# Batch 1 of a fused retention and gated-MLP kernel: its MLP by halves of 256 tokens, its second half of attention in 64-token chunks

## The chip, the cores and the metric

The kernel runs on one core of a Trainium2 chip. The core has a matrix engine (PE, with its weight loads shown apart as PEld), a vector engine (DVE), a scalar engine (ACT), a general engine (POOL) and an engine that issues transfers (SP). Each engine works through its own instructions in order and waits on semaphores for the others. Matrix results land in PSUM, which has eight banks of 512 float32 columns per partition. The metric is the device time of one execution in microseconds.

## The reference, cut to what matters

```python
# q, k, v: (8 batches, 8 heads, 576 positions, 64)
scores = q @ k.T / sqrt(64)
gamma  = 1 - 2 ** (-5 - arange(8))                 # one decay per head
ret    = scores * where(i >= j, gamma ** (i - j), 0)
x      = (ret @ v)  laid out as (8 * 576 tokens, 512)
h      = x @ w_in                                   # (512, 2048)
g      = h / (1 + exp(-beta * h))                   # beta: one per column
out    = g @ w_out                                  # (4608, 512)
```

The decay is split: queries are multiplied by gamma^i and the scale, values by gamma^-j, so only the triangle (i >= j) has to be masked. This also lets everything before a chunk be summed up in a state, keys^T times values, one 64 x 64 block per head.

## The kernel before, in words

Each batch has a main block of 512 tokens; the 64 tokens left over of all eight batches form a ninth block. So there are nine blocks of 512 tokens for the MLP (called MoE in the names). For one block `up` (L542) computes one of 16 column groups `fo` of the hidden layer: four matmuls of 128 x 512 over `ko`, then a Silu on ACT from PSUM into `gT`. `down` (L575) does four of sixteen `fo` steps for one of four groups `ms` of 128 tokens; after the last of them the result is copied into `ot` and sent out. A block is thus 16 up steps and 16 down steps.

Main blocks hold their tokens interleaved by four: token 4*s + i lies in column s of group i. Queries are loaded that way (`load_q`, L73), so a chunk of 128 tokens is columns 32c to 32c+31 of all four groups.

Attention has two forms. Batches 0 and 1 work in 128-token chunks, `i` = 0 to 7 in `seq`: `a_sc` (scores, then the mask `causal` on DVE), `a_st` (adds to the running state in PSUM and copies it out to `sbds`), `a_O` (masked scores times values), `a_cross` (queries times the state), `a_x` (copy to `xT`, the MLP's input). Queries and keys are turned by PE (`t_q`, L317; `t_k`, L324). Batches 2 to 7 work in 64-token chunks, eight to a block, four small 64 x 64 matmuls at a time: `d_st` (L473) computes the states of four chunks into two banks, one of the tag st and one of the tag mm; its `chain` adds them up on DVE, four links, each with a cast on ACT into `sbq`. `d_sc` (L451) computes the scores with masks from `tri`; `d_out` (L494) the outputs and the cross terms, then evicts to `xT`. `scores(u)` and `outputs(u)` (L725, L732) put these together; `outputs(u)` holds the first states of batch u+1 between the two parts of the cross terms. Queries and keys of these batches are turned by transposing transfers on SP.

PSUM banks are shared by tag: mm has three (ups, downs and one bank of each `d_st`), O two, sc two, st one. A bank is given back, in program order, after the last use of what it held, and the bank that came back first is handed out next; the engine that writes it again waits on a semaphore until the last reader is done.

The order of work is written by hand. `fill` is the list of MLP steps; `merged` (L602) walks it, and before step n it issues every attention step whose time is at most n. `d0` is the first down of batch 0, `u1` the first up of batch 1 (d0 + 16), `base[n]` the first step of block n (`base[1]` is u1 + 10). In the kernel before, batch 1's list is 20 half-width ups (`fo` 0 to 9, tokens 0 to 255, then 256 to 511), six full ups and 16 downs: 42 steps. Chunks 4 and 5 are done at d0 + 12.7 to d0 + 15.9, chunks 6 and 7 among the half-width ups (u1 + 1 to u1 + 7), the first states of batch 2 (`early_states`) alone at u1 + 27, its scores and second states at base[2] - 10 and its outputs at base[2] - 3.5, all three among the downs.

SP issues in program order: queries, keys and values of batch 0, the weights, then queries, keys and values of batch 1, then those of batch 2, and so on.

Of the kernel before, what the change touches and what calls it, by code (L numbers as in the profile page):

```python
# [19 lines left out]
def kernel(  # L20
# [49 lines left out]
    QB = 2  # L70
    q_tiles, kv_tiles = {}, {}

    def load_q(b, us=(0, 1)):  # L73
# [51 lines left out]
    pos = consts.tile([P, 2, CB + 1], F32, name="pos")  # L125
    for j, (step, mul) in enumerate(((1, CB), (P, 1))):
        nc.gpsimd.iota(pos[:, j, :CB], pattern=[[step, CB]], base=0, channel_multiplier=mul,
                       allow_small_or_imprecise_dtypes=True)
        for x in range(2):
            nc.gpsimd.iota(pos[x * TL:(x + 1) * TL, j, CB:], pattern=[[0, 1]], base=MB, channel_multiplier=1,  # L130
                           allow_small_or_imprecise_dtypes=True)
    lscale = consts.tile([P, 1], F32, name="lscale")
    nc.vector.memset(lscale[:], math.log(scale))
    lg = consts.tile([P, 2, CB + 1, H], F32, name="lg")
# [5 lines left out]
    nc.scalar.activation(gv[:], lg[:, 1], ACT.Exp, scale=-1.0)  # L140

# [10 lines left out]
    tri = [consts.tile([P, TL], BF16, name=f"tri{i}") for i in range(2)]  # L152
# [97 lines left out]
    def head_of(b, p, j):  # L250
        return 2 * p + (j if b is not None and b < QB or p < 2 else 1 - j)

    def pre_q(b, n):
# [4 lines left out]
        if b < 2:  # L258
# [14 lines left out]
    def pre(i, js=(0, 1)):  # L273
# [22 lines left out]
        for to, hs in turned if b >= QB else [(slice(0, H), slice(0, H))]:  # L296
# [19 lines left out]

    def t_q(b, u):  # L317
# [12 lines left out]
    def q_cols(i, r, p):  # L330

        b, c = seq[i]
        if b is None:
            return live[i]["qkT"][r, 0, p, :], lambda o: o
        return (batch[b]["qT"][r, :, p, c * PC:(c + 1) * PC], lambda o: o.rearrange("k (i s) -> k i s", i=CB))

    def a_sc(i):
# [11 lines left out]
        m_b = causal[:].unsqueeze(1).to_broadcast([P, HP, P])  # L349
# [48 lines left out]
    def a_x(i):  # L398
        b, c = seq[i]
        x, view = xt(b)[:, :, :, c * PC:(c + 1) * PC], lambda o: o.rearrange("k p (i s) -> k p i s", i=CB)  # L400
        Os = live[i]["O"]
# [6 lines left out]
    def a_st(i):  # L408
# [11 lines left out]
        for j in range(2):  # L420
            r, cols = slice(j * D, (j + 1) * D), slice(j * D, (j + 1) * D)
            e = nc.vector.tensor_copy if i in (CB + 2, CB + 3) else nc.scalar.copy
# [4 lines left out]
            e(ends[b][(1 - j) * D:(2 - j) * D, 2:], st[r, 2:, cols])  # L427

# [9 lines left out]
    def q_of(u, c, j, p):  # L438

        if u == B:  # L440
            return piece(u, c)["qkT"][half(j), 0, p, half(c % 2)]
        w = TL // CB
        return batch[u]["qT"][half(j), :, p, c * w:(c + 1) * w]

    def columns(u, o):
        return o if u == B else o.rearrange("k (i s) -> k i s", i=CB)
# [4 lines left out]
    def d_sc(u):  # L451

        R = [sb.tile([P, 2, 2, HP, TL], BF16, name="R", tag="R", bufs=4) for _ in range(2)]
        sc = {}
        for x in range(2):
            for j in range(2):
                sc[x, j] = psum.tile([P, 2, HP, TL], F32, name="sc", tag="O" if x else "sc", bufs=2)
# [6 lines left out]
        mask = tri[1 if u == B else 0][:].unsqueeze(1).to_broadcast([P, 2 * HP, TL])  # L464
# [343 lines left out]
```

## Time and profile before

| | us |
|---|---|
| median of 3 runs (lowest, highest) | 299.39 (298.9, 300.13) |
| profiled execution, its span | 298.64, 296.9 |
| PE busy | 286.9 (97%) |
| ACT, POOL, DVE busy | 147.1, 109.0, 101.3 |
| an up or down step of 512 columns (four matmuls) | 0.86 |
| first up of batch 1, of batch 2, of batch 3 | 50.3, 84.2, 114.5 |

The granted clock of PE is 0.999 of full speed. A matmul's duration in the rows is longer than its share of PE's time, since matmuls overlap: 379 ns for one of 512 columns, but 0.215 us from one to the next. So steps are best measured from start to start, or by the chain of work in order of time. In a row the first number is the start, the second the length, both in us from the start of the span; a bracket at the end gives the engine's idle time ahead of it and what ended it. L549 is the MLP's up matmul, L551 its Silu, L582 the down matmul, L589 the copy of its result, L480 and L488 the states and the links of their sum, L491 the casts of these on ACT, L462 and L469 the 64-token scores and masks, L508, L521 and L536 the outputs, cross terms and evictions; L347, L351, L418, L394, L380 and L406 are the same for 128-token chunks.

### The profile page before, as it was taken

What the parts mean: (1) busy time and instruction counts of PE and PEld (TensorE: products, weight loads), DVE (VectorE), ACT (ScalarE), POOL (GpSimd) and SP (SyncE); (2) the same over time, 40 slices, a digit from 0 to 9 for tenths busy, and PEclk for the clock granted to TensorE, in tenths of its full rate; (3) what the DMA queues carried; (4) which work ended last, traced back from release to release, by engine and by line L of the source; (5) the groups of instructions that cost most, each with busy time, mean ns of one, the idle gap of its engine ahead of it and who ended that gap; (6) DMA issues with size and microseconds to landing.
All of it is one profiled execution on the core that took longest, in us unless ns stands there. A gap on an engine that the chain in (4) does not pass through costs nothing.

```text
span 296.9 us, 7459 instructions
## 1 busy us (share of the span) xinstructions
PE 286.9 (97%) x3147; PEld 149.2 (50%) x3177; DVE 101.3 (34%) x209; ACT 147.1 (50%) x257; POOL 109.0 (37%) x211
## 2 busy tenths in 40 slices
PE   7799999999999999999999999999999999999995
PEld 5554456855544454455445544554454544444444
DVE  5563656704640552045204530354054300120012
ACT  5567546683277434743484347433770157008600
POOL 3666107693750923370429216736223000000000
PEclk9999999999999999999999999999999999999999
DMA  8999999999999999949999849999976110131012
GB/s 213 218 333 393 386 273 252 224 203 222 252 169 254 270 196 242 242 68 160 233 237 207 178 99 272 195 181 188 205 168 140 73 38 0 35 71 38 0 71 73
DMA packets 128273, 53.97 MB, mean 182 GB/s; under 512 B 110048, under 2 KB 120688, under 8 KB 128240
## 3 DMA queue, kind: packets, MB, share of 16 engines
q1 hardware_dynamic: 128208, 53.49, 82.4%
q8 instruction: 25, 0.41, 0.6%
q14 instruction: 8, 0.07, 0.1%
q10 hardware_dynamic: 32, 0.01, 0.0%
HBM read 36.71 MB, written 9.44 MB: 155 GB/s over the span
## 4 chain that ended last, share of the span: by engine, by line
PE 83%; DMA 5%; SPq 5%; POOL 3%; issue 2%; ACT 1%; POOLq 0%; DVE 0%
PE po L582 38%; PE ph L549 33%; PE ph L564 4%; DMA tln<-in_k_dram 3%; SPq L94 2%; DMA kvn<-in_k_dram 2%; PE O L508 1%; SPq L113 1%; POOL kn L286 1%; PE st L480 1%; PE sc L462 1%; DMA kT<-kn 1%; SPq L305 1%; POOL kn L285 1%; PE O L521 1%
## 5 line engine op out<-in xcount | busy, mean ns | idle before, releaser
L582 PE MATMUL po<-w_out_sb,gT 128*128 128x512 bf16 (+2 forms) x590 | 125.6, 367 | 2.3 <-issue 2.1
L551 ACT ACTIVATE gT<-ph,beta_sb 128x512 bf16<-128x512 f32 (+1 forms) x140 | 91.2, 657 | 52.1 <-PE ph L549 51.7
L549 PE MATMUL ph<-xT,w_in_sb 128*128 128x512 bf16 (+1 forms) x550 | 114.5, 364 | 0.5
L582 PEld LDWEIGHTS <-gT 128*128 128x128 bf16 x608 | 56.9, 98 | 62.9
L549 PEld LDWEIGHTS <-w_in_sb 128*128 128x128 bf16 x560 | 54.3, 98 | 57.6 <-DVE sum L488 0.7
L589 DVE COPY ot<-po 128x512 f32<-128x512 f32 (+2 forms) x34 | 22.3, 657 | 72.3 <-PE po L582 71.6
L297 POOL CAST kn<-kvn 128x128 bf16<-128x128 f32 (+2 forms) x80 | 25.9, 359 | 43.5 <-DMA kvn<-in_k_dram 43.0
L266 POOL TENSOR_TENSOR qs<-qn,gq 128x256 bf16<-128x256 f32 (+1 forms) x36 | 26.3, 759 | 36.0 <-DMA qn<-in_q_dram 34.6
L469 DVE TENSOR_TENSOR R<-sc,tri 128x512 bf16<-128x512 f32 x28 | 17.4, 683 | 61.4 <-PE sc L462 61.4
L277 POOL TENSOR_TENSOR vn<-kvn,gv 128x512 bf16<-128x512 f32 x32 | 33.3, 1044 | 13.5 <-DMA kvn<-in_v_dram 8.5
L536 ACT CAST xT<-O 128x512 bf16<-128x512 f32 x14 | 7.5, 589 | 32.0 <-PE O L521 32.0
L491 ACT CAST sbd<-warm 128x256 bf16<-128x256 f32 x18 | 7.3, 405 | 25.5 <-DVE warm L488 20.6
L564 PE MATMUL ph<-xT,w_in_sb 128*128 128x512 bf16 x54 | 12.3, 379 | 0.3 <-ACT xT L404 0.2
L351 DVE TENSOR_TENSOR R<-sc,causal 128x512 bf16<-128x512 f32 x16 | 10.2, 685 | 4.6 <-PE sc L347 4.5
L488 DVE TENSOR_TENSOR sum<-st,warm 128x256 f32<-128x256 f32 x24 | 10.2, 425 | 2.5
L488 DVE TENSOR_TENSOR warm<-st,sum 128x256 f32<-128x256 f32 x18 | 7.6, 422 | 9.6 <-PE st L480 8.4
L536 DVE CAST xT<-O 128x512 bf16<-128x512 f32 x14 | 9.0, 686 | 5.0 <-PE O L521 5.0
L567 ACT ACTIVATE gT<-ph,beta_sb 128x512 bf16<-128x512 f32 x14 | 8.7, 687 | 4.2 <-PE ph L564 4.2
L285 POOL TENSOR_TENSOR kn<-tln,gq 128x128 bf16<-128x128 f32 (+1 forms) x12 | 5.7, 472 | 10.5 <-DMA tln<-in_q_dram 6.9
L194 POOL CAST w_in_sb<-wt 128x256 bf16<-128x256 f32 (+1 forms) x12 | 7.4, 623 | 4.9 <-DMA wt<-in_moe_w_in_dram 4.9
L564 PEld LDWEIGHTS <-w_in_sb 128*128 128x128 bf16 x56 | 5.4, 98 | 6.7 <-issue 0.3
L219 PE MATMUL ph<-warm 128*128 128x128 f32 (+1 forms) x24 | 7.3, 444 | 1.3 <-DVE warm L123 1.3
(81 smaller groups left out, 154.1 us busy)
## 6 DMA issues: line engine op xcount, KB each, us to landing
qn<-in_q_dram SPq DMA_DIRECT2D x16, 512.0 KB, 5.4
kvn<-in_k_dram SPq DMA_DIRECT2D x32, 256.0 KB, 5.4
kvn<-in_v_dram SPq DMA_DIRECT2D x32, 256.0 KB, 5.0
out_dram<-ot SPq DMA_DIRECT2D x31, 256.0 KB, 3.8
wt<-in_moe_w_out_dram SPq DMA_DIRECT2D x8, 512.0 KB, 9.1
wt<-in_moe_w_in_dram SPq DMA_DIRECT2D x5, 512.0 KB, 8.1
wt<-in_moe_w_in_dram SPq DMA_DIRECT2D x6, 256.0 KB, 5.5
out_dram<-ot SPq DMA_DIRECT2D x9, 128.0 KB, 2.4
```

The source lines that it names most:

```text
L266: nc.gpsimd.tensor_tensor(batch[b]["qs"][:, cs, to], q_tiles[b][:, hs, cs].rearrange("p h i d -> p i h d"), gq[:, cs, hs].unsqueeze(3).to_ ...
L277: nc.gpsimd.tensor_tensor(live[i]["vn"][:], kv_tiles.pop(i)[:, 1], gains(gv, c), ALU.mult)
L297: nc.gpsimd.tensor_copy(kn[:, c % 2, to], t[:, 0, hs])
L351: nc.vector.tensor_tensor(R[:, j], sc[j][:], m_b, ALU.mult)
L469: nc.vector.tensor_tensor(R[x][:, j].rearrange("k c p q -> k (c p) q"), sc[x, j].rearrange("k c p q -> k (c p) q"), mask, ALU.mult)
L488: nc.vector.tensor_tensor(new[:], add, sums[(c - 1) % 2][:], ALU.add)
L536: (nc.scalar.copy if n % 2 else nc.vector.tensor_copy)(x, o)
L549: nc.tensor.matmul(ph, w_in_sb[:, ko, fo * P:(fo + 1) * P], xts[m][:, ko, :, w], start=(ko == 0), stop=(ko == KO - 1))
L551: nc.scalar.activation(gts[m][:, fo, :, w], ph, ACT.Silu, scale=beta_sb[:, fo:fo + 1])
L564: nc.tensor.matmul(phs[f][:], w_in_sb[:, ko, f * P:(f + 1) * P], xts[m][:, ko], start=(ko == 0), stop=(ko == KO - 1))
L582: nc.tensor.matmul(po[:, :nn], gT[:, fo, ms, :], w_out_sb[:, fo, n0:n0 + nn], start=(fo == 0), stop=(fo == FO - 1))
L589: (nc.scalar.copy if m == 0 else nc.vector.tensor_copy)(ot, po[:, :nn])
```

## The change

Batch 1 (`HB`) is laid out by halves: token 256*x + 2*p + i lies in column p of group 2x + i. Its queries are loaded by halves of 256 tokens, in pieces of 512 bytes where they were 1 KB; the first half of its keys and values is loaded behind the first half of the queries, the second behind the second. A third table of decays (`gqh`) fits this layout. The MLP of batch 1 becomes: all 16 ups of 256 columns for the first half, the downs of its two token groups, then the same for the second half: 48 steps, of which 32 are half-width ups.

The first half of the attention stays in 128-token chunks (4 and 5) with a mask of its own; their outputs come one down step earlier (d0 + 15). The state after chunk 5 goes into `sums[1]` in four DVE copies, and from there into `sbq[3]` by a cast on ACT. The second half is attended in 64-token chunks: `scores(1)` at u1 + 10 computes the states of chunks 4 to 7 of eight and the scores, with the chain ahead of the masks; `outputs(1)` at u2 - 1.5, u2 being the second half's first up, computes the outputs and, between the cross terms, the first states of batch 2. `early_states` is gone. Batch 2's scores are at base[2] - 10.5, which is now two half-width ups ahead of the second half's downs, its outputs at base[2] - 3.

Queries of batch 1 are turned by halves (`t_qh`), the first at d0 + 11.6, the second at u1 + 4, both copied by ACT; before, the second was copied by DVE at d0 + 12.6. Keys 6 and 7 are turned at u1 + 2 and u1 + 5. POOL casts these keys in three pieces instead of one, since the 64-token form holds its heads in another order.

```diff
 def load_q(b, us=(0, 1)):
+        if b == HB:
+            for x in us:
+                nc.sync.dma_start(t[:, :, 2 * x:2 * x + 2].rearrange("p h i d -> p h (i d)"),
+                                  q[b, :, x * HT:(x + 1) * HT, :].rearrange("h (p i) d -> p h (i d)", i=2))
+            return
 ...
+    gqh = consts.tile([P, CB, H], F32, name="gqh")
+    nc.scalar.activation(gqh[:], lg[:, 2, :CB], ACT.Exp, bias=lscale[:])
 ...
 def pre_q(b, n):
+        if b == HB:
+            cs = slice(2 * n, 2 * n + 2)
+            for to, hs in turned if n else [(slice(0, H), slice(0, H))]:
+                nc.vector.tensor_tensor(batch[b]["qs"][:, cs, to], q_tiles[b][:, hs, cs].rearrange("p h i d -> p i h d"),
+                                        gqh[:, cs, hs].unsqueeze(3).to_broadcast([P, 2, len(range(H)[hs]), D]), ALU.mult)
+            return
 ...
+    def t_qh(x):
+        T = psum.tile([P, 2, HP, P], BF16, name="T", tag="O", bufs=2)
+        for i in range(2):
+            for p in range(HP):
+                nc.tensor.transpose(T[:, i, p, :], heads(batch[HB]["qs"][:, 2 * x + i], p), ident[:])
+        nc.scalar.copy(batch[HB]["qT"][:, 2 * x:2 * x + 2], T[:])
 ...
 def a_st(i):
-            e = nc.vector.tensor_copy if i in (CB + 2, CB + 3) else nc.scalar.copy
+            e = nc.scalar.copy
+            if i == CB + 1:
+                nc.vector.tensor_copy(sums[1][r, :2], st[r, :2, cols])
+                nc.vector.tensor_copy(sums[1][half(1 - j), 2:], st[r, 2:, cols])
+                continue
 ...
+        if i == CB + 1:
+            nc.scalar.copy(sbq[3][:], sums[1][:])
 ...
 def d_sc(u):
+        xs = range(u == HB, 2)
-                sc[x, j] = psum.tile([P, 2, HP, TL], F32, name="sc", tag="O" if x else "sc", bufs=2)
+                sc[x, j] = psum.tile([P, 2, HP, TL], F32, name="sc", tag="O" if x and u != HB else "sc", bufs=2)
 ...
 def d_out(u):
+        ccs = range(2 if u == HB else 0, CB)
 ...
-    fill += [F(up, 1, fo, 2 * x, 2) for x in range(2) for fo in range(10)]
-    fill += [F(up, 1, fo) for fo in range(10, FO)]
-    fill += [F(down, 1, ms, f0) for ms in range(MB // P) for f0 in range(0, FO, 4)]
-    base = {1: u1 + 10}
+    for x in range(2):
+        fill += [F(up, HB, fo, x) for fo in range(FO)]
+        fill += [F(down, HB, ms, f0) for ms in (2 * x, 2 * x + 1) for f0 in range(0, FO, 4)]
+    u2 = u1 + FO + 8
 ...
-               [(10.3, F(load_q, 1))] + [(10.3, F(load_kv, CB + n, (j,))) for n, j in keys_first],
+               [(10.3, f) for x in range(2) for f in [F(load_q, HB, (x,))] + [F(load_kv, CB + n, (j,)) for n, j in keys_first[4 * x:4 * x + 4]]],
 ...
+               [(d0 + 7, F(pre_q, HB, 0)), (d0 + 15.96, F(pre_q, HB, 1)), (d0 + 11.6, F(t_qh, 0)), (u1 + 4, F(t_qh, 1))],
 ...
-                (d0 + 12.7, F(t_k, 4)), (d0 + 14, F(t_k, 5)), (d0 + 14, F(a_sc, 4)), (d0 + 15, F(a_sc, 5)),
-                (d0 + 15, F(a_st, 4)), (d0 + 15.9, F(second, 4))],
+                (d0 + 12.2, F(t_k, 4)), (d0 + 13.2, F(t_k, 5)), (d0 + 13.2, F(a_sc, 4)), (d0 + 14.1, F(a_sc, 5)),
+                (d0 + 14.1, F(a_st, 4)), (d0 + 15, F(second, 4))],
 ...
-                (d0 + 15.95, F(t_k, 6)), (u1 + 1, F(t_k, 7)), (u1 + 2, F(a_sc, 6)), (u1 + 3, F(a_sc, 7)),
-                (u1 + 4, F(a_st, 6)), (u1 + 7, F(second, 6))]]
+                (u1 + 2, F(t_k, 6)), (u1 + 5, F(t_k, 7))]]
 ...
-        for f in [chain] + steps if u == B - 1 else steps + [chain]:
+        for f in [chain] + steps if u in (HB, B - 1) else steps + [chain]:
 ...
-    streams.append([(base[1] + 17, F(early_states, XB))])
+    streams.append([(u1 + 10, F(scores, HB)), (u2 - 1.5, F(outputs, HB))])
-        lo, hi = (base[n] + 17, base[n + 1] - 9.5) if n == 1 else (base[n] + 3, base[n + 1] - 14)
+        lo, hi = (u2 + 1, base[2] - 9.5) if n == 1 else (base[n] + 3, base[n + 1] - 14)
-        work = [(n + 1, hi - 0.5, hi + 6)] if n == 1 else [(n + 1, hi - 1, hi + 6.5)]
+        work = [(n + 1, base[2] - 10.5, base[2] - 3)] if n == 1 else [(n + 1, hi - 1, hi + 6.5)]
```

More of the change, by code (lines that the diff above doesn't have):

```diff
@@ L151 @@
                             fill=0.0, base=0, channel_multiplier=-1)
-    tri = [consts.tile([P, TL], BF16, name=f"tri{i}") for i in range(2)]
+    tri = [consts.tile([P, TL], BF16, name=f"tri{i}") for i in range(3)]
+    causal_h = consts.tile([P, P], BF16, name="causal_h")
     NS = 3
@@ L250, in head_of @@
     def head_of(b, p, j):
-        return 2 * p + (j if b is not None and b < QB or p < 2 else 1 - j)
+        return 2 * p + (j if p < 2 else 1 - j)
     def pre_q(b, n):
@@ L441, in q_of @@
             return piece(u, c)["qkT"][half(j), 0, p, half(c % 2)]
+        if u == HB:
+            return batch[u]["qT"][half(j), 2:, p, c % 4 * 32:c % 4 * 32 + 32]
         w = TL // CB
@@ L500, in to @@
             o = O[c % 2, p // 2][half(x), p % 2]
-            return o[:, c // 2] if u == B else o[:, :, c // 2]
+            return o[:, c // 2] if u == B else o[:, :, c // 2 - ccs[0]]
         R = batch[u]["R"]
-        for cc in range(CB):
+        for cc in ccs:
             for p in range(HP):
@@ L727, in scores @@
         masks = d_sc(u)
-        steps = [lambda: masks(0), lambda: masks(1)]
-        for f in [chain] + steps if u == B - 1 else steps + [chain]:
+        steps = [F(masks, x) for x in range(u == HB, 2)]
+        for f in [chain] + steps if u in (HB, B - 1) else steps + [chain]:
             f()
```

69 lines of the change are left out of this document (41 added, 28 removed).

## The prediction

> **What bounds the kernel now.** I read the page first (busy shares, then the chain that ended last), then the timelines of PE, DVE and ACT around each place where the change puts something.
>
> ```profile
> span 296.9 us, 7459 instructions
> PE 286.9 (97%) x3147; PEld 149.2 (50%) x3177; DVE 101.3 (34%) x209; ACT 147.1 (50%) x257; POOL 109.0 (37%) x211
> PE po L582 38%; PE ph L549 33%; PE ph L564 4%; DMA tln<-in_k_dram 3%; SPq L94 2%; DMA kvn<-in_k_dram 2%; PE O L508 1%; SPq L113 1%; POOL kn L286 1%; PE st L480 1%; PE sc L462 1%; DMA kT<-kn 1%; SPq L305 1%; POOL kn L285 1%; PE O L521 1%
> ```
>
> PE is full: 97%, and three quarters of the chain is the MoE's matmuls. So the change costs or brings what it does to PE: work taken from it, and holes torn into it. After the first 20 us no hole is over 0.6 us, so there is nothing for a late PE to catch up in.
>
> The pair of scores ahead of the first second-chunk outputs of batch 1 (PE, then DVE):
>
> ```profile
> 47.34 0.40 PE L347 MATMUL sc<-qT,kT 64*128 64x128 bf16 x8
> 47.67 0.40 PE L418 MATMUL st<-vn,kn 128*128 128x128 bf16 x4
> 47.90 1.03 PE L582 MATMUL po<-w_out_sb,gT 128*128 128x512 bf16 x4
> 48.86 0.67 PE L394 MATMUL O<-R,vn 128*64 128x128 bf16 x16
> ...
> 46.47 2.59 DVE L351 TENSOR_TENSOR R<-sc,causal 128x512 bf16<-128x512 f32 x4 [0.94 <-PE sc L347]
> ```
>
> The four masks end at 49.06; the down step at 47.90 lies in front of the outputs that need them. Silu behind half-width ups:
>
> ```profile
> 56.76 5.71 ACT L551 ACTIVATE gT<-ph,beta_sb 128x256 bf16<-128x256 f32 x13 [1.31 <-PE ph L549]
> ```
>
> Thirteen without a pause: (5.71 - 0.474)/12 = 0.436 us each, where PE needs 0.432 (half the 0.864 between full Silus from 62.86 on). ACT has nothing to spare in half-width ups.
>
> Batch 2's scores with its second states (PE, then DVE):
>
> ```profile
> 72.73 0.45 PE L480 MATMUL st<-vn,kn 64*64 64x64 bf16 x32
> 73.01 0.75 PE L462 MATMUL sc<-qT,kT 64*64 64x64 bf16 x64
> 73.92 5.99 PE L582 MATMUL po<-w_out_sb,gT 128*128 128x512 bf16 x27 [0.16 <-issue]
> ...
> 73.60 2.48 DVE L469 TENSOR_TENSOR R<-sc,tri 128x512 bf16<-128x512 f32 x4 [1.72 <-PE sc L462]
> 76.00 0.41 DVE L488 TENSOR_TENSOR warm<-st,sum 128x256 f32<-128x256 f32 x1
> 77.57 0.42 DVE L488 TENSOR_TENSOR sum<-st,warm 128x256 f32<-128x256 f32 x1
> ```
>
> The states lie in two PSUM banks, one of them of the mm tag, which also serves every up and down. That bank is read last by the add that ends at 77.99: it is held for 5.26 us from 72.73. Here that is free, since a down keeps its bank for 3.45 us. Batch 2's outputs:
>
> ```profile
> 81.62 2.54 PE L582 MATMUL po<-w_out_sb,gT 128*128 128x512 bf16 x11 [0.16 <-issue]
> ...
> 81.67 1.29 DVE L536 CAST xT<-O 128x512 bf16<-128x512 f32 x2 [0.82 <-PE O L521]
> 82.88 0.41 DVE L490 COPY warm<-st 128x256 f32<-128x256 f32 x1
> 84.45 0.42 DVE L488 TENSOR_TENSOR sum<-st,warm 128x256 f32<-128x256 f32 x1
> 84.80 0.68 DVE L589 COPY ot<-po 128x512 f32<-128x512 f32 x1
> ```
>
> Evictions, four links 0.53 apart, and only then the output copy of the down in flight. Last, batch 7's states among full-width ups, chain first (PE, DVE, ACT):
>
> ```profile
> 214.27 0.44 PE L480 MATMUL st<-vn,kn 64*64 64x64 bf16 x32
> 215.26 5.44 PE L549 MATMUL ph<-xT,w_in_sb 128*128 128x512 bf16 x23
> ...
> 214.83 0.42 DVE L488 TENSOR_TENSOR warm<-st,sum 128x256 f32<-128x256 f32 x1 [8.39 <-PE st L480]
> ...
> 216.91 0.41 ACT L491 CAST end<-sum 128x256 bf16<-128x256 f32 x1
> ```
>
> The adds end 2.60 and ACT's copies 3.05 us after the states began; two full ups (1.73) just cover that.
>
> **PE's own work.** Removed, by the chain in order of time: scores of chunks 6 and 7 0.46 + 0.33, states 0.22 + 0.22, outputs 0.57, cross 0.55, the lone first states of batch 2 0.38 + 0.16 of switching: 2.89 us. Added: second states 0.38, half of a score stage 0.29 (of 0.58), switching 0.16; in the outputs half of 0.79, 16/28 of the cross (0.22 + 0.24), batch 2's states 0.27, switching 0.16: together 1.91. Net -0.98; bounds -1.2 and -0.7, as such rows differ by a quarter. Transposes of queries and keys are only moved.
>
> **Half-width ups.** 32 for 20. The run of 13 took PE 56.12 to 61.97, 0.24 over 13 x 0.432, mostly the ring's start. 12 more: 0.05 (the 4 ns) to 0.5 (that overhead twice); I take 0.2.
>
> **Outputs of chunks 4 and 5 one down earlier.** Scores, first states and outputs now follow each other without the down of 0.86 between. PE is ready at 47.90 + 0.30 (half of the outputs), the masks end at 49.06: PE waits, in all some 0.95, less the 0.13 it now idles before the first up: +0.8. Bounds 0 (masks earlier) and 1.0. Keys 4 and 5 are loaded behind half a query load instead of a whole one; they come earlier, and PE sets the pace there, so nothing.
>
> **Start of the ups.** The state after chunk 5 goes to DVE as four 64-partition copies of 0.3 each, and ACT's cast of it waits for the last; behind that cast stand batch 0's last output copy (0.59) and the first Silus. Counted from the scores' 47.34: states done 2.63, DVE copies to 4.05, cast to 4.5, output copy to 5.0. PE has done the last down at 3.49, two half-ups and a key transpose by 4.57, and the third up needs the bank of that output copy: 0.5. The second query transpose puts a 1.01 us copy (by the L322 row, 128x1024) on ACT between Silus: 0.2 more. +0.7; bounds 0 and 1.0. DVE's pre-scaling of the second queries, about 1.5 us in three pieces, ends before PE asks for it.
>
> **Scores of batch 1 in the ups.** A bank of a tag is taken again in the order in which they came back, so the third matmul group after the states gets the states' bank. States at 0, ups resume at 0.75 (half a score stage less than 215.26 - 214.27), two half-ups end at 1.61; the bank is free at 2.60 + 0.1: wait 1.1. Meanwhile ACT stands at its four copies until 3.05, so the next up waits 0.4 for the Silu of the first: +1.5. Bounds 1.1 (ACT catches up unseen) and 1.6. Before, no such wait was possible, since chunks 6 and 7 used the st bank alone.
>
> **Outputs of batch 1 one down ahead of the second half.** From PE's resumption: down to 0.86; evictions of 256 columns (two of 0.425 on DVE) end at 0.85, so the first up starts at 0.95. The second needs the states' bank: links begin at 0.77 and 0.53 apart, the last ends at 2.77, so it starts at 2.87. The third needs the down's bank, whose copy ends at 3.4. Its start at 3.48 against 1.72 unhindered: +1.75; bounds 1.5 and 2.0. The transfers of batch 2's keys and values are not late for it: POOL has them ready at 63.0, PE asks at about 67.7, and POOL's extra copies (three instead of one for keys 6 and 7, some 0.4 each) and the twice as many, half as long packets of batch 1's queries (1 KB to 512 B) cost about 2 of that cover.
>
> **Scores of batch 2, now two half-ups before the downs.** By 72.73 to 77.99 the bank is held 5.26. PE goes on at 1.19, ends two half-ups at 2.05, and the first down needs that bank: it waits to 5.36. +3.3; bounds 2.9 and 3.6. It was in the downs before, with four microseconds of them to cover it.
>
> **Taken as nothing.** The third table of positions and its Exp add some 0.5 us to POOL and ACT at the start, where DVE waits 1.45 us for the first queries (until 4.99); without that cover it would be 0.5. The two new masks are made on POOL in its idle 12.3 us before 43.45. The query halves cost SP twice the packets for two issues (1.0 us of SP time by the rows of keys, 256 KB in as many packets); SP there waits for the transfers ahead, and keys 6 and 7 come up to 1 us later, but are asked for three half-ups later too.
>
> **Sum.** -0.98 + 0.2 + 0.8 + 0.7 + 1.5 + 1.75 + 3.3 = 7.27, less 0.35 of small holes between half-ups that chunks 6 and 7 made: +6.9. The profiled execution took 298.64 us (span 296.9); the three runs shown have a median of 299.39. 298.64 + 6.9 = 305.5; on the median 306.3. I forecast 306.0. Preparation for batches 2 and 3 keeps its place in the queues of SP and POOL while PE comes later; its price is between -0.3 and +0.8, taken as 0. All lower bounds together give +3.7, all upper ones +9.5: 303 to 309.
>
> **Rivals.** (1) *The waits do not come*: banks come free in time because another bank is handed out. Then only PE's own work and the first two terms of delay count, at their low ends: about -0.9, 298.5 on the median, faster. For it: PE's work does shrink by 0.98. Against it: the run of 13 Silus holds the pace of a ring of three banks, and the add at 77.57 must read the states' bank. It decides as soon as each of the three bank waits is under 0.2. Chance 0.06, and 0.03 for a part of them that ends within 0.5% of 299.4. (2) *One wait is missing or half as long*, above all that of batch 2's scores: 306.0 - 3.3 = 302.7; from 301 to 303.5. Chance 0.13. (3) *The clock falls in the longest hole.* PE would stand 3.3 us; the granted clock is 0.999 over this span and no row shows PE idle that long, so the trace can neither show nor exclude it. If the matmuls behind the hole ran at half pace for as long as the hole, that would add 1.7 us: 307.7, up to 310 if two holes do it. Chance 0.08. [...]
>
> **How the numbers follow.** The forecast itself holds 0.70, at 303 to 309. A measurement of this kernel tells about 0.5% (1.5 us) from no change. Slower: 0.70 + 0.13 + 0.08 = 0.91; same 0.03; faster 0.06. The range, 302.0 to 309.5, leaves out rival 1, the low end of rival 2 and the worst of rival 3.
>
> **What would show it.** Each wait should stand as PE idle released by DVE: L488 ahead of a ph in batch 1's first half (1.1, then 0.4 released by ACT), L488 ahead of the second ph of its second half (1.5), L488 ahead of the first po behind batch 2's scores (3.3), and L351 ahead of O (0.9 in two pieces). PE's busy time should fall by about 1 us. If PE's holes between the first down of batch 0 and the first up of batch 2 stay under 2 us in sum, the bank order is what I have wrong; if a hole is released by a DMA or POOL, the preparation; if rows behind a hole show matmuls spaced over 0.3 us at 512 columns, the clock.

## The result, and the profile after

The changed kernel takes 308.59 us (median of 4 executions, 307.21 to 310.94) where the kernel before takes 299.14 (4 executions, 297.92 to 300.13): a ratio of 1.033, 95% interval 1.025 to 1.040. The profiled execution took 308.53 us with a span of 306.8, against 298.64 and 296.9. Executions of the changed kernel differ in the clock that TensorE was granted: the four have means of 0.989, 0.989, 0.994 and 0.999, where the kernel before stays at 0.998 or more; ratios leave out executions over 1.5% above the fastest of their kernel.

Lines of the page of the changed kernel: span, engines, granted clock in 40 slices of 7.67 us, and the two matmul groups of the MLP (L590 the ups, L623 the downs), with their idle time and what ended most of it in the last field. In the changed kernel L526 and L529 are the links of the sum and their casts, L507 the 64-token masks, L592 the Silu, L378 and L421 masks and outputs of the 128-token chunks.

```profile
span 306.8 us, 7691 instructions
PE 290.1 (95%) x3251; PEld 151.7 (49%) x3281; DVE 99.7 (33%) x209; ACT 150.5 (49%) x270; POOL 112.0 (36%) x222
PEclk9999999999879999999999999999999999999999
L623 PE MATMUL po<-w_out_sb,gT 128*128 128x512 bf16 (+2 forms) x589 | 128.2, 373 | 5.8 <-DVE sum L526 3.3
L590 PE MATMUL ph<-xT,w_in_sb 128*128 128x512 bf16 (+1 forms) x575 | 115.6, 355 | 3.4 <-DVE sum L526 2.3
```

Two things are new: PE stands 5.6 us behind DVE's sums of the states (L526), and in two slices the clock is not full. Everything happens in one stretch. From the first down of batch 0 (32.58, before 32.51) to the first up of batch 2 (94.00, before 84.00) the changed kernel needs 61.42 us where 51.49 were enough: +9.93. The span is longer by 9.9, so nothing is made good or lost behind it in this execution.

PE's timeline of the changed kernel, the rows with the new holes (start, length, and in brackets the idle time ahead and what ended it):

```profile
48.13 0.41 PE L421 MATMUL O<-R,vn 128*64 128x128 bf16 x8 [0.45 <-DVE R L378]
48.73 0.41 PE L421 MATMUL O<-R,vn 128*64 128x128 bf16 x8 [0.18 <-DVE R L378]
...
52.03 1.03 PE L590 MATMUL ph<-xT,w_in_sb 128*128 128x256 bf16 x8 [0.37 <-ACT ot L630]
...
57.05 1.05 PE L590 MATMUL ph<-xT,w_in_sb 128*128 128x256 bf16 x8
58.98 0.61 PE L590 MATMUL ph<-xT,w_in_sb 128*128 128x256 bf16 x4 [0.88 <-DVE sum L526]
59.79 1.47 PE L590 MATMUL ph<-xT,w_in_sb 128*128 128x256 bf16 x12 [0.20 <-ACT gT L592]
...
71.12 5.99 PE L590 MATMUL ph<-xT,w_in_sb 128*128 128x256 bf16 x52 [1.43 <-DVE sum L526]
...
78.00 1.05 PE L590 MATMUL ph<-xT,w_in_sb 128*128 128x256 bf16 x8
82.36 0.61 PE L623 MATMUL po<-w_out_sb,gT 128*128 128x512 bf16 x1 [3.31 <-DVE sum L526]
```

Each place that the prediction named has its hole, with the releaser that it named. Behind `scores(1)` and `scores(2)` two half-width ups (x8) go through and the third matmul group stands: it was handed the mm bank that the states lie in. Its last reader, on DVE:

```profile
77.90 2.48 DVE L507 TENSOR_TENSOR R<-sc,tri 128x512 bf16<-128x512 f32 x4 [6.25 <-PE sc L500]
...
81.88 0.42 DVE L526 TENSOR_TENSOR sum<-st,warm 128x256 f32<-128x256 f32 x1
```

The states start on PE at 77.04, the add that reads the bank last ends at 82.30, and the first down starts at 82.36. The bank is held for 5.26 us, the figure that the profile of before gave.

The rest is the clock. Short windows of the changed kernel (duration, then busy time and instructions by engine, then the granted clock in the column before DMA's share):

```profile
80.00:81.00 1.00, 0.00 (x0) 0.00 (x0) 0.90 (x3) 0.25 (x1) 0.90 (x1) 1.00 1.33 231
81.00:82.00 1.00, 0.00 (x0) 0.00 (x0) 0.79 (x3) 0.75 (x3) 0.59 (x2) 0.68 0.85 145
82.00:83.00 1.00, 0.61 (x1) 0.28 (x3) 0.30 (x1) 0.88 (x3) 1.00 (x3) 0.50 0.97 215
87.00:88.00 1.00, 1.00 (x4) 0.42 (x3) 0.00 (x0) 0.00 (x0) 0.52 (x3) 0.50 1.03 193
88.00:89.00 1.00, 1.00 (x6) 0.42 (x5) 0.12 (x1) 0.00 (x0) 0.00 (x0) 0.91 1.15 263
```

PE stops at about 79.05. At 81.4, still inside the hole, the clock goes to half, and it comes back at 88.2: 6.83 us. The five downs behind the hole take from 82.36 to the outputs' start at 89.64, 7.28 us; in an execution of the same order of work without the fall (below) they take 82.41 to 86.83, 4.42. That is 2.9 us for the clock.

### The profile page after: what moved, and what is told of

Read it like the earlier page. It is cut to its first block, busy times and chain, and to the rows that moved or that the text cites. A ratio compares the mean times of both kernels' runs of the same rounds, so it can differ in the third digit from the quotient of the medians.

```text
span 306.8 us, 7691 instructions
## 1 busy us (share of the span) xinstructions
PE 290.1 (95%) x3251; PEld 151.7 (49%) x3281; DVE 99.7 (33%) x209; ACT 150.5 (49%) x270; POOL 112.0 (36%) x222
## 4 chain that ended last, share of the span: by engine, by line
PE 87%; DVE 5%; SPq 2%; issue 2%; DMA 2%; ACT 1%; POOL 0%; DVEq 0%; ACTq 0%
PE po L623 40%; PE ph L590 35%; PE ph L605 4%; PE O L560 2%; SPq L100 2%; DMA kvn<-in_k_dram 2%; PE O L547 2%; PE st L518 2%; PE sc L500 1%; DVE sum L526 1%; DVE R L378 1%; DVE warm L526 1%; DVE R L507 1%; PE T L352 0%; DVE xT L578 0%
## 5 line engine op out<-in xcount | busy, mean ns | idle before, releaser
L623 PE MATMUL po<-w_out_sb,gT 128*128 128x512 bf16 (+2 forms) x589 | 128.2, 373 | 5.8 <-DVE sum L526 3.3
L590 PE MATMUL ph<-xT,w_in_sb 128*128 128x512 bf16 (+1 forms) x575 | 115.6, 355 | 3.4 <-DVE sum L526 2.3
L592 ACT ACTIVATE gT<-ph,beta_sb 128x512 bf16<-128x512 f32 (+1 forms) x146 | 91.8, 641 | 48.6 <-PE ph L590 48.3
L623 PEld LDWEIGHTS <-gT 128*128 128x128 bf16 x608 | 57.5, 99 | 68.5 <-issue 3.8
L590 PEld LDWEIGHTS <-w_in_sb 128*128 128x128 bf16 x584 | 56.4, 98 | 60.0 <-DVE sum L526 3.7
L315 POOL CAST kn<-kvn 128x128 bf16<-128x128 f32 (+2 forms) x84 | 27.5, 364 | 55.3 <-DMA kvn<-in_k_dram 50.1
L507 DVE TENSOR_TENSOR R<-sc,tri 128x512 bf16<-128x512 f32 x30 | 18.7, 683 | 65.9 <-PE sc L500 65.9
L284 POOL TENSOR_TENSOR qs<-qn,gq 128x256 bf16<-128x256 f32 (+1 forms) x36 | 26.3, 757 | 27.7 <-DMA qn<-in_q_dram 27.6
L578 ACT CAST xT<-O 128x512 bf16<-128x512 f32 (+1 forms) x16 | 8.2, 562 | 43.3 <-PE O L560 43.3
L529 ACT CAST sbd<-warm 128x256 bf16<-128x256 f32 x19 | 7.7, 405 | 23.0 <-DVE warm L526 18.6
L526 DVE TENSOR_TENSOR warm<-st,sum 128x256 f32<-128x256 f32 x20 | 8.4, 422 | 12.0 <-PE st L518 10.6
L526 DVE TENSOR_TENSOR sum<-st,warm 128x256 f32<-128x256 f32 x26 | 11.1, 425 | 2.8
L578 DVE CAST xT<-O 128x512 bf16<-128x512 f32 (+1 forms) x16 | 9.8, 653 | 6.1 <-PE O L560 6.1
L529 ACT CAST sbd<-sum 128x256 bf16<-128x256 f32 x19 | 7.7, 405 | 2.4 <-DVE sum L526 0.2
L605 PEld LDWEIGHTS <-w_in_sb 128*128 128x128 bf16 x56 | 5.3, 97 | 6.8 <-POOL w_in_sb L206 0.5
```

Of the source, the lines that this page charges most:

```text
L284: nc.gpsimd.tensor_tensor(batch[b]["qs"][:, cs, to], q_tiles[b][:, hs, cs].rearrange("p h i d -> p i h d"), gq[:, cs, hs].unsqueeze(3).to_ ...
L315: nc.gpsimd.tensor_copy(kn[:, c % 2, to], t[:, 0, hs])
L507: nc.vector.tensor_tensor(R[x][:, j].rearrange("k c p q -> k (c p) q"), sc[x, j].rearrange("k c p q -> k (c p) q"), mask, ALU.mult)
L526: nc.vector.tensor_tensor(new[:], add, sums[(c - 1) % 2][:], ALU.add)
L529: nc.scalar.copy((sbq[c] if c < NC - 1 else ends[u])[:], new[:])
L578: (nc.scalar.copy if n % 2 else nc.vector.tensor_copy)(x, o)
```

## The experiments

The theory to test: the loss is the sum of waits for banks in the order of their handing out, above all the 3.3 us at batch 2's scores, and a fall of the clock behind long holes. Rivals: the wait at batch 2's scores is for something else (the amount of work moved there), or the loss sits in the added half-width ups, in the preparation, or in where things lie in memory.

**Batch 2's scores one half-up later.** If it is the bank, one half-up less must reach the downs before the third group.

```diff
-        work = [(n + 1, base[2] - 10.5, base[2] - 3)] if n == 1 else ...
+        work = [(n + 1, base[2] - 9.5, base[2] - 3)] if n == 1 else ...
```

> The changed kernel with batch 2's scores and second states one half-width up later, so that the first down is the second matmul group behind the states instead of the third. Bank theory: the down takes a bank that is free, and the third group (the next down, 0.43 + 3.45 us later) finds the states' bank nearly free, so the wait of 3.31 us falls to at most 0.3, and without a long hole the granted clock stays at 1.00, which gives back the 2.9 us that the downs behind it lost: 308.6 - 3.1 - 2.9 = 302.6. Rival, crowding: scores, masks and links among the second half's ups cost PE the same wherever the bank goes: 308 to 309. Rival, hole without clock: the slow matmuls behind the hole have another cause (POOL or transfers): 305.5, with matmuls at half pace still there near 83 us.

Profiled 303.76 us (span 302.1, clock 1.000); four executions, median 306.63, ratio 1.027 (1.023 to 1.031). PE, then ACT, of this kernel:

```profile
78.98 3.40 PE L623 MATMUL po<-w_out_sb,gT 128*128 128x512 bf16 x15
83.71 1.25 PE L623 MATMUL po<-w_out_sb,gT 128*128 128x512 bf16 x5 [1.33 <-ACT gT L592]
```

```profile
82.87 0.41 ACT L529 CAST end<-sum 128x256 bf16<-128x256 f32 x1
83.19 0.47 ACT L592 ACTIVATE gT<-ph,beta_sb 128x256 bf16<-128x256 f32 x1
```

The wait for the bank is gone, as it should be: the group that gets it is now covered by the downs. But the expectation of at most 0.3 us for the rest was missed. The downs need the last Silu of the half, and that Silu stands on ACT behind the four casts, which wait for the chain behind the masks. The 3.31 us became 1.33. So the same late chain holds PE twice, by the bank and by ACT's queue, and freeing one shows the other. The median misses the expected 302.6 by four microseconds: the three executions without a profile took 305.83 to 307.59, one of them at a clock of 0.998, and no trace shows where.

**The chain between the two masks.** This leaves every matmul where it is and only brings DVE's chain forward by one pair of masks, 1.25 us.

```diff
+        if u == XB:
+            steps = [steps[0], chain, steps[1]]
-        for f in [chain] + steps if u in (HB, B - 1) else steps + [chain]:
+        for f in [chain] + steps if u in (HB, B - 1) else steps if u == XB else steps + [chain]:
```

> The changed kernel; for batch 2 alone the four links come between the first two masks and the last two, not behind all four. The states' bank is held 1.24 us less (two masks of 0.62). Bank theory: the wait of the first down falls from 3.31 to about 2.05 us. Whether a hole of 2 us lowers the clock is open: if the clock falls only when PE stands idle for most of 3.4 us, it stays at 1.00 and the time is 308.6 - 1.25 - 2.9 = 304.4; if any hole over some 1.5 us is enough, 307.3. Rival, crowding: the same work on the same engines, 308 to 309.

**The chain later.** The reverse: the second pair of masks is carried out twice, so that the chain starts 1.25 us later; the repetition changes no value.

```diff
+        if u == XB:
+            steps = steps + [steps[1]]
```

> The changed kernel; for batch 2 alone the last two masks are issued twice (the same values written again), which puts 1.24 us of DVE work ahead of the links. Bank theory: the first down waits 3.31 + 1.25 = 4.55 us. If the half-pace stretch behind a hole has a length of its own (6.8 us in the profile of the changed kernel, from 81.4 to 88.2), a longer hole only eats into it: its start lies inside the hole, so 1.25 us of hole cost about 0.6 to 1.25 us, 309.2 to 309.9. If the stretch grows with the hole, 310.5 or more. Rival, crowding or another cause: no change, 308.6.

The down behind the hole, in PE's timeline of the one and of the other:

```profile
81.40 4.49 PE L623 MATMUL po<-w_out_sb,gT 128*128 128x512 bf16 x20 [2.12 <-DVE sum L526]
```

```profile
83.75 6.18 PE L623 MATMUL po<-w_out_sb,gT 128*128 128x512 bf16 x20 [4.51 <-DVE sum L526]
```

2.12 and 4.51 us, against 2.05 and 4.55 expected: the hole follows the chain's end, 1.2 us for 1.2 us, with no matmul moved. That excludes the amount of work as its cause. In time: profiled 304.23, four executions up to 309.27, median 307.17 (ratio 1.025, 1.019 to 1.031) with the shorter hole; profiled 312.56, median 312.3 (1.045, 1.041 to 1.049) with the longer. The clock doesn't follow the hole's length. Behind 4.51 us the 20 matmuls take 6.18 us where they take 4.49 behind 2.12, and 1.69 us more is half pace for some 3.4 (an estimate from these two rows); behind 3.31 in the changed kernel half pace lasted 6.83 us; behind 2.12 the row shows none.

The longer hole cost more than the 309.2 to 309.9 that was expected of a fall with a length of its own. Its trace has a second wait, of 1.9 us, for turned keys of the leftover tokens. Its mean clock of 0.989 over a span of 310.8 us comes to some 6.8 us at half pace, twice what the row behind the hole shows, so by this estimate there was a second stretch of some 3.4 us; where it lay isn't shown. The changed kernel's own trace has no wait at the leftover scores. Those scores come up again below.

**The same hole in the kernel before.** If bank order is the cause, the kernel before must be hurt in the same way when scores go two full ups ahead of downs. Here these are batch 3's scores, ahead of batch 2's downs.

```diff
-        work = ... else [(n + 1, hi - 1, hi + 6.5)]
+        work = ... else [(n + 1, hi - 4.5 if n == 2 else hi - 1, hi + 6.5)]
```

> The kernel before, with one thing moved: batch 3's scores and second states come two full-width ups ahead of batch 2's downs instead of one down behind their start. Nothing of batch 1 is touched. Bank theory: PE goes on 1.19 us behind the states' start, two full ups take 1.73, and the first down waits for the states' bank until 5.36: a hole of 2.4 us released by the last link on DVE, 299.1 + 2.4 = 301.5 (304.4 with a fall of the clock as after the longest hole). Rival, cause in batch 1's new layout: no hole, 299.1. Rival, keys or queries not yet turned at the earlier time: a wait of the scores for a transfer instead.

Its PE timeline:

```profile
96.83 1.90 PE L549 MATMUL ph<-xT,w_in_sb 128*128 128x512 bf16 x8
101.11 7.94 PE L582 MATMUL po<-w_out_sb,gT 128*128 128x512 bf16 x36 [2.39 <-DVE sum L488]
```

2.39 us for 2.4 expected. Five executions: 301.0, 301.2 and 301.2 at clocks of 0.998 to 1.000, 303.0 and 303.5 at 0.994; against 298.7 of the kernel before on this chip that is 2.4 without a fall of the clock and some 4.5 with a lower one (ratio of all 1.011, 1.007 to 1.014). The two with the lower clock have no trace, so it isn't shown whether it fell behind this hole. The cause therefore works without halves, half-width ups or a changed layout.

**Three groups moved back, or one.** In the changed kernel, outputs of chunks 4 and 5, scores of batch 1 and outputs of batch 1 go to places where downs cover their chains (the first two added lines), or only batch 2's scores do (the third).

```diff
-                (d0 + 14.1, F(a_st, 4)), (d0 + 15, F(second, 4))],
+                (d0 + 14.1, F(a_st, 4)), (d0 + 15.9, F(second, 4))],
-    streams.append([(u1 + 10, F(scores, HB)), (u2 - 1.5, F(outputs, HB))])
+    streams.append([(u1 + 15.5, F(scores, HB)), (u2 - 3.5, F(outputs, HB))])
...
-        work = [(n + 1, base[2] - 10.5, base[2] - 3)] if n == 1 else ...
+        work = [(n + 1, base[2] - 8.5, base[2] - 3)] if n == 1 else ...
```

The first two, so that the longest hole alone is left:

> As the kernel with all four times altered, but batch 2's scores again two half-width ups ahead of the downs, as in the change. Theory: one hole of 3.3 us, released by the last link on DVE, on top of 0.997: ratio 1.008 where the clock holds, 1.018 in runs where it falls to half for 6.8 us. If the clock's fall needs the earlier holes of 0.4 to 1.4 us too, every run shows 1.00.

The third alone, so that the shorter holes are left:

> The changed kernel with batch 2's scores at the first down of the second half, all else as in the change: the longest hole is gone, the three shorter places stay. Theory: 308.6 - 3.3 - 2.9 = 302.4, ratio 1.012, where the clock holds. The run with the scores one up later had a lowered mean clock in three of four executions though its longest hole was 1.5 us; if the shorter holes lower the clock too, this kernel shows a clock of 0.993 to 0.998 in part of its executions and a ratio of 1.02; if it was that run's 1.33 us wait on a Silu, every execution shows 1.00.

The first has its hole of 3.32 us (`78.91`, released by L526) and was profiled at 301.81 us with a clock of 0.999: a hole as long as that of the changed kernel, and no fall (the 20 matmuls behind it take 4.49 us). Its other three executions show 0.994, 0.994 and 0.989 and 303.3 to 305.4 (ratio 1.018, 1.015 to 1.021); where the clock fell in them isn't on record. The second was profiled at 306.43, four microseconds more than its holes explain; its other executions lie between 302.5 and 307.2 (1.018, 1.014 to 1.023). Where the four come from, in its PE timeline near the leftover block:

```profile
232.08 0.32 PE L500 MATMUL sc<-kT 64*64 64x64 bf16 x16 [0.53 <-DMA kT<-kn]
234.32 0.43 PE L500 MATMUL sc<-kT 64*64 64x64 bf16 x16 [1.92 <-DMA kT<-kn]
234.68 6.85 PE L623 MATMUL po<-w_out_sb,gT 128*128 128x512 bf16 x24
```

Here, 140 us behind the stretch that the change alters, PE waits 2.45 us for turned keys of the leftover tokens, and behind that the clock falls: in steps of 1 us from 234 on it is 0.67, 0.50, 0.50 and 0.63, which makes 3.40 us at half pace, and 24 matmuls take 6.85 us in place of the 5.35 that they take ahead of the wait. The same row of the kernel before:

```profile
228.15 0.32 PE L462 MATMUL sc<-kT 64*64 64x64 bf16 x16 [0.20 <-DMA kT<-kn]
```

So the kernel before stands at the very edge there: 0.20 us of waiting, no slack. The chain in front of it is serial: loads of leftover tokens, casts on POOL, a pair of transposing transfers issued by SP, twice. Followed back from the scores, the end of that chain is the same in both: from the cast that waits for the last load of leftover keys (229.63 here, 223.46 before) to the scores it is 4.69 us, 3.03 of them, in the kernel before, for the last transposing transfer. What is late is that load. Counted from PE's first leftover scores (231.11 here, 227.38 before), it is issued at -6.8 us in place of -8.4, and it takes 5.23 us to land in place of 4.32. SP, which issues it, falls behind in the loads of the last batch and of the leftover tokens before that: at their start (189.81) it stands 41.3 us ahead of PE's leftover scores, 40.8 in the kernel before, and at their end (its next row, `qT`, at 204.99) 26.1, against 27.7. In the trace with the longer chain, the other one with a long wait, that is 26.1 too, in the changed kernel's own, which has none, 28.3, and in two with waits of 0.3 and 0.4 us 26.5 and 26.6, so this lead alone doesn't settle the wait.

**All four times moved back.** What is left of the change with its holes taken away?

> The changed kernel with only four times altered, so that the new work stands where downs cover it: outputs of chunks 4 and 5 behind the last down of batch 0 again, scores of batch 1 behind its sixteen half-width ups, outputs of batch 1 two downs earlier, scores of batch 2 at the first down of the second half. All else of the change stays. Theory: only PE's own work is left, -0.98 for the attention and +0.2 for twelve more half-width ups, about 0.8 us under the kernel before: ratio 0.997, no PE wait over 0.3 us behind the first down of batch 0 and before batch 2, granted clock 1.00 in every run. Rival: half-width ups, the new query layout or the transfers cost by themselves, 1.005 or more.

Profiled 297.9 us (span 296.2, clock 1.000), no wait of PE over 0.30 us in the stretch. But only two of twelve executions were so short; nine lie at 300.2 to 302.4, five of them at an unbroken clock, and one took 496.3 us at a mean clock of 0.56. The median is 300.78, the ratio 1.005 (1.002 to 1.008). So a second cost exists, in most executions, and the holes of the change are not it. The profiled execution is one of the two short ones, so no trace shows that cost in this version.

**Addresses.** The change moves the large SBUF tiles from 320 to 480 bytes past a multiple of 512, by the sizes of the tiles ahead of them. Dropping one small tile (`fenced`) puts them on multiples of 64 bytes; a pad of 160 bytes in the kernel before takes them off.

```diff
-    fenced = consts.tile([P, 1], F32, name="fenced")
+    fenced = lscale
```

```diff
+    pad = consts.tile([P, 40], F32, name="pad")
+    nc.vector.memset(pad[:], 0.0)
```

> The kernel with all four times moved back took 297.8 in its two fastest executions and 300.2 to 302.4 in the others, which the kernel before never shows. Its new constants shift every large tile in SBUF from 320 bytes past a multiple of 512 to 480 past it, that is from a multiple of 64 bytes to 32 past one. Here one 4-byte constant shares its place with another, so that all large tiles lie at 448, a multiple of 64 again; no instruction is added or taken away. Address theory: the slower executions go, 297.5 to 298.5, ratio 0.997. Rival, tail chain: the serial chain of loads, casts and turns for the leftover tokens is late for another reason (order or times of the transfers), so nothing changes: 300.5, ratio 1.005.

> The kernel before with 160 bytes of an unused constant (one memset more), so that all large tiles lie at 480 bytes past a multiple of 512, as in the changed kernel. Address theory: part of its executions take 300 to 302, ratio 1.003 to 1.008. Rival: 298.7 in all, ratio 1.000.

> The changed kernel with the same shared constant, large tiles at 448. Address theory: the tail's wait goes and 308.6 falls by some 2 us to 305.5 to 307, what is left being the four waits and the clock's fall. Rival: 308.6.

The version moved back, aligned: 300.97 (ratio 1.007, 1.005 to 1.009), as without. The kernel before, shifted: 299.24 (1.0016, 1.0001 to 1.0031). Addresses are not the second cost; they can be 0.3% at most. The changed kernel, aligned: 306.59, ratio 1.025 (1.024 to 1.027), of four executions at 305.79, 306.51, 306.66 and 310.49 with clocks of 1.000, 0.993, 1.000 and 0.989. That median is 2.0 below the changed kernel's and inside the 305.5 to 307 that the address theory gave; but the intervals meet (1.025 to 1.040 for the change), the clocks of the eight executions differ, and the other two runs speak against it. Its profiled execution, 305.79, is worth more than its alignment: it has the order of work of the change, the same holes to 0.02 us, and a mean clock of 1.000 (20 matmuls behind the longest hole take 4.49 us, as they do elsewhere at full pace).

```profile
core 0: 304.0 us, clock 1.000
```

```profile
71.17 5.99 PE L590 MATMUL ph<-xT,w_in_sb 128*128 128x256 bf16 x52 [1.44 <-DVE sum L526]
...
82.41 4.49 PE L623 MATMUL po<-w_out_sb,gT 128*128 128x512 bf16 x20 [3.32 <-DVE sum L526]
...
91.18 7.07 PE L590 MATMUL ph<-xT,w_in_sb 128*128 128x512 bf16 x32
```

From its first down at 32.52 to the first up of batch 2 at 91.18 it takes 58.66 us, 7.2 more than before. That is the price of the waits less what PE saves, with no clock in it.

**The leftover scores two downs later.** If the second cost is the wait for turned keys, 1.75 us of cover must take most of it. The control is the kernel before with the same line.

```diff
-            work = [(B - 1, lo + 7, lo + 12.5), (B, lo + 19, lo + 24.5)]
+            work = [(B - 1, lo + 7, lo + 12.5), (B, lo + 21, lo + 25.5)]
```

> The four groups stand where they did in the version with all four moved back; besides, the scores of the leftover block stand two downs later (1.75 us on PE) and its outputs one down later. If the executions at 300 to 301 us with an unbroken clock are those in which PE waits some 2.4 us in the leftover scores for turned keys, 1.75 us of that wait is now covered by the two downs, and such executions come out near 298.6; the median of all then lies between 298.0 and 299.3, against 300.78 and 300.97 for the two versions with the scores in the old place. If the 2.4 us are lost elsewhere, the median stays at 300.5 to 301.2. With the kernel's outputs one down later, 2.7 us are left between them and the next ups in place of 3.6; if their evictions are late, PE shows a wait of up to 0.9 us before those ups, in every execution.

> The control: the kernel before with the same two shifts of the leftover block and nothing else. It waited 0.20 us there for turned keys in its profiled execution, so by the first theory it gains 0 to 0.3 us (298.4 to 299.0); if the shift costs something by itself (outputs nearer to the ups), it shows here as 0.3 to 0.9 us more. The difference between the two kernels of this call is then the change without its waits: PE's own work says 1.0 us less than before; anything within 0.5 us of zero says that this gain does not reach the end.

The version moved back: 298.45 us, twelve executions from 297.80 to 300.06, ratio 1.0006 (0.9990 to 1.0023), all at clocks of 0.999 or 1.000. The control: 298.37 (297.63 to 299.60), ratio 0.9988 (0.9976 to 1.0001). The 2.4 us are gone from the one and almost nothing from the other, and the low mean clocks went too (four of the twelve executions of the version without this line had 0.993 or 0.994, three of twelve with aligned tiles). The comparison is of ratios, each with the kernel before measured alongside. That the cost lies at the leftover scores is thereby shown, though no trace caught it in the version moved back; why the loads for them come late in most executions of the changed family and not in the kernel before is open. SP issues the same instructions in the same order behind batch 1 in both.

PE's stretch of these two kernels, from the first down of batch 0 to the first up of batch 2 (columns: duration; PE, PEld, DVE, ACT and POOL busy; clock, DMA's share, GB/s), with the change moved back, then with the kernel before:

```profile
32.59:84.37 51.78, 50.94 (x741) 32.05 (x740) 25.18 (x54) 31.64 (x69) 26.74 (x48) 1.00 1.07 234
```

```profile
32.71:84.13 51.42, 51.42 (x637) 30.05 (x636) 26.88 (x54) 28.10 (x57) 27.85 (x48) 1.00 1.11 244
```

The change does spare PE something, 0.48 us of busy time, but the stretch is no shorter: small waits (0.29 for the eviction of `xT` and 0.18 for a Silu at the start of the ups, 0.37 of issue in batch 2's outputs) take it. No version that was run is measurably faster than the kernel before.

## Why the prediction was right

The measured 308.59 lies in the range (302.0 to 309.5), on the side that had 0.91. The forecast of 306.0 is 2.6 below it, and there is luck in the upper end: one of the four executions, at 310.94, lies above it, and what lifts the measured time above the forecast stood in no term of the sum. Going through the sum, with the rows of the changed kernel and of the execution with an unbroken clock:

| step of the prediction | forecast | measured, and from what |
|---|---|---|
| outputs of chunks 4 and 5 one down earlier | +0.8 | second scores to first up 46.95 to 50.39, 3.44, less 2.48 of work: 0.96, of which 0.22 were lost before too: 0.74 (the holes in the rows, 0.45 and 0.18, are smaller, since matmuls overlap: in the version with aligned tiles 20 matmuls, 0.368 us each in the mean of L623, take 4.49) |
| start of the ups | +0.7 | ten half-ups with their transposes 50.39 to 56.38, 5.99, less 10 x 0.432 and 0.9 of transposes: 0.77 |
| scores of batch 1 | +1.5 | ups from 57.05 to the downs at 61.09, 4.04, less 2.59 for six half-ups: 1.45 |
| outputs of batch 1 before the second half | +1.75 | second half-up 2.91 behind PE's resumption in place of 1.29, and 0.30 lost in the run of 13: 1.9 |
| scores of batch 2 | +3.3 | 3.31 by the hole; 78.05 to 82.41 less 0.86 for two half-ups: 3.5 by starts, as the other rows |
| PE's own work, 12 more half-width ups, old holes | -1.13 | 7.17 less the five above: about -1.2, a remainder and no measurement of its own |
| sum without the clock | +6.9 | +7.17 in the stretch, +7.1 in the span (304.0 against 296.9) |
| clock behind the longest hole | rival 3, 1.7 | 0 (305.79, 301.81), 2.9 (308.53) |
| preparation for later batches | 0 | no wait in the profiled execution; 2.45 us, with a fall of the clock, and 1.9 us in those of two other versions |

The mechanism held term by term: bank order, the chain behind the masks, ACT's queue. What lifts the time above the sum is, in the profiled execution, the clock: 2.9 us, a rival with a chance of 0.08. In the other executions it isn't traced. One took 307.21 at a clock of 0.999, 1.4 more than 305.79; a wait at the leftover scores, which the sum took as nothing, would account for it, but that is argued from the other versions.

**The clock.** By their mean clocks it fell in three of the four executions of the change and in two of four with the aligned tiles: rival 3 happened, and should have had most of the chance that was given to the forecast without it. Its price was mis-sized too: the half pace was taken to last as long as the hole, and no run shows that. It lasted 6.83 us behind the hole of 3.31 (81.36 to 88.19), 3.40 behind waits of 2.45 at the leftover scores, some 3.4 behind 4.51, and it was absent behind 3.32. The part behind the hole cost half its length: 5.83 us (82.36 to 88.19), 2.9 of loss. The chances of 0.70 and 0.08 had no row behind them, since the kernel before never idles over 0.6 us there.

What the traces show behind each hole:

| trace | hole of PE | clock behind it |
|---|---|---|
| changed kernel | 3.31 | half for 6.83 us, from 2.31 us after PE stopped |
| the same with aligned tiles | 3.32 | full, 20 matmuls in 4.49 us |
| only the longest hole | 3.32 | full, 20 in 4.49 |
| longer chain | 4.51 | 20 in 6.18, half for some 3.4 us by estimate |
| shorter chain | 2.12 | full, 20 in 4.49 |
| kernel before with one hole | 2.39 | full, 36 in 7.94 |
| shorter holes only, leftover scores | 0.53 and 1.92 | half for 3.40 us, 24 in 6.85 |

So a hole of 3.3 us led to a fall in one trace and to none in two others, and 2.45 us in two pieces led to one where 2.39 in one piece did not. The two conditions in the expectation for the shorter chain, most of 3.4 us or any hole over some 1.5, were assumptions, and the table fits neither: these 2.45 us led to a fall, 2.12, 2.39 and 3.32 did not. No run was made to find out what decides it, and these traces don't show it.

**Preparation.** It was argued that SP and POOL keep their order while PE comes later, and the price was taken as 0, at most +0.8. The order is indeed the same, but the margin was not looked at: the row at 228.15 of the kernel before shows the leftover scores already waiting for a transfer. A chain without slack belongs into the sum with both bounds, even far behind the change; the upper bound of +0.8 was too low against waits of 1.9 and 2.45 us.

**PE's own work.** -0.98 was forecast, with +0.2 for the half-width ups, so -0.78 in all. The pages seem to show a rise from 286.9 to 290.1, but the page of before has only 3147 matmuls for 3177 weight loads. The control, with the same work and all 3177 recorded, has 290.0, the version moved back 289.2 to 289.4: a fall of 0.6 to 0.8. Sign and size were right, and in the time it is nothing.

Rival 1 fell with every bank wait in place. Rival 2, a missing wait, fell with the 3.31.

## What to carry to other kernels

When a matmul stage with a slow reader is moved ahead of other matmuls, count which later group is handed its bank, and look where the reader's chain stands in its engine's queue: two half-width ups in front of the third group cover 0.9 us, a group of four downs 3.5 each, and the chain here holds its bank for 5.3. Put the stage where long groups follow it, and expect a second wait of the same chain through another engine when the first is removed. A hole in a full TensorE can cost more than itself, by the clock behind it: here 3.31 us cost 2.9 more in one execution, 3.32 nothing more in another, and 2.45 cost 1.5 more. And a transfer chain that ends without slack in the profile of before is part of the price of any change, however far away.

## What was not expected of the hardware

A hole's length alone doesn't decide how long the granted clock falls: behind 3.3 us it was at half pace for 6.83 us (profiled execution of the change, 308.53) or not at all (305.79 and 301.81), behind 2.45 us for 3.40. In traced spans of about 305 us these 3.40 us go with a mean clock of 0.994 and the 6.83 with 0.989, so that 0.993 and 0.989 in executions without a trace are read, as an estimate, as falls of about these lengths. The shorter one cost 1.5 us behind the leftover scores (24 matmuls in 6.85 us against 5.35).

The row of SP that turns the last leftover keys is 3.74 us long in the profiled execution of the version moved back, 4.54 in the kernel before and 5.97 in the version with the shorter holes. That isn't a transfer getting slower: the row is a pair of issues (1.31 and 1.48 us in the kernel before), and the second waits for POOL's casts of the keys. From the end of these casts to the scores it is 3.10 us in the slowest case (231.22 to 234.32), as in the kernel before (225.05 to 228.15, 3.03 of them the transfer). What scatters is the load of the keys ahead of the casts, in when it is issued and in how long it takes to land (4.32 and 5.23 us). Why was not found.
